# Packed attention and channel mixer: keys and queries turned by TensorE, scores and packed values in small tiles, w1 float32 on chip, the folded w1 made 512 columns ahead

## The chip, the cores and the metric

The kernel runs on one core of one Trainium2 chip. The metric is the device time of one execution in microseconds (us). Engines are TensorE (PE; PEld is its weight load), VectorE (DVE), ScalarE (ACT), GpSimd (POOL) and SyncE (SP), whose queue issues all transfers here.

## The reference

```python
def _attn_ref(q, k, v, p):             # 8 batches, 8 heads, 576 tokens, 64 wide; p has 32 packs
    scale = 1.0 / np.sqrt(q.shape[-1])
    def sm_attn(qq, kk, vv):
        s = scale * np.matmul(qq, kk.transpose(0, 1, 3, 2))
        a = np.exp(s - np.max(s, axis=-1, keepdims=True))
        a = a / (np.sum(a, axis=-1, keepdims=True) + 1e-09)
        return np.matmul(a, vv)
    p_packed = sm_attn(p, k, v)
    return sm_attn(q, p_packed, p_packed)

def _moe_ref(x, U, V, w_ch1, w_ch2):   # x: 8 x 576 x 512; U 576 x 32, V 32 x 576
    h = x.transpose(0, 2, 1) @ U @ V
    u = x + h.transpose(0, 2, 1)
    return u + np.maximum(u @ w_ch1, 0.0) @ w_ch2    # w_ch1 512 x 2048, w_ch2 2048 x 512
```

U, V and the two weights reach the kernel as 64-bit floats and are turned into 32-bit ones on the chip.

## The kernel before

**Two stages.** The opening works in 16 units, (batch, half of the heads). It loads k and v, turns k, makes the scores of the packs against the keys, the softmax and the packed values (`ppall`). After `actx.close()` the order is written out by hand: a loop over the 8 batches, and in each over 16 blocks of 128 hidden columns (kt).

**The folded w1.** The second attention gives weights `a` over 32 packs for each of 8 heads. Since x = a times pp, the product pp w1 (256 x 2048 for each batch, "the fold" here) takes the place of w1, and gemm1 multiplies the 256 attention weights per token with it, then gemm2 multiplies the relu with w2.

**Two kinds of multiplication.** `mm3` splits both operands into a float32r high part and the rest, and runs three float32r matmuls. Plain float32 operands are given to TensorE as they are.

**The opening, unit u.** `a_load` fetches k in a layout in which VectorE's 32x32 transpose (`transposed`, L101) can turn it; `a_split` builds block diagonals of p (`bdp`, L313); `a_scores` runs four float32 matmuls of 288 columns against the block diagonal (L322); `a_softmax` takes maximum and Exp (L330, L332); `a_turn` turns the exponentials on TensorE (L342); `a_pack` multiplies all four heads' values at once and picks the diagonal (L358, L362). Between, `convert_w1` makes w1 float32 (L67 to L71), `split_w1` splits it (L123, L124), and `fold` multiplies pairs of heads by w1 for batches 0 to 3 and stores them in DRAM (`wsr`, L393). A scheduler places these instructions on each engine.

**The batch loop.** Each kt has gemm1 (L632, halves of 256 and 320 tokens, evicted by L638 on ScalarE and L640 on VectorE) and gemm2 of the block before (L649). Every second kt `load_wt` fetches 256 folded columns from DRAM and `split_wt` splits them (L452, L453). `attention(b + 2)` is a list of steps of which one runs per kt: turning q on VectorE (L101), splitting it (L180, L181), scores in `mm3` against block diagonals (L192), softmax, turning back (L225), the mixers with U and V (L236, L249). `later` makes the fold for batches 4 to 7 in the loop (L592) and stores it (`wsc`). The last 64 tokens of two batches share one product (`joint`). In batch 0, w2 is converted, one block a kt. TensorE's transposes and `psT`'s two PSUM banks serve all steps of the loop.

## Time and profile before

| | before |
|---|---|
| median of three runs | 874.17 us (870.17 to 874.59) |
| the profiled execution | 876.01 us |
| its span, first to last instruction | 874.2 us |
| granted TensorE clock, mean | 0.982 |
| TensorE busy | 95% |
| VectorE, ScalarE, GpSimd busy | 59%, 43%, 30% |
| moved by DMA | 98.55 MB |

The span is what the trace shows; the execution's own time has 1.8 us around it. Matmuls are pipelined: a record starts before the one ahead of it has ended, so what a matmul costs on TensorE is the distance between two starts, not its duration. Rows of the timeline give start, duration, engine, line, operation and tile ("out<-in"); rows of groups give busy time and mean duration, then the idle time ahead of the group and what ended it.

### The profile page before, as it was taken

Reading aid. Unit: us, or ns where it says so; the run is one execution under the profiler, and the core shown is the slowest. Engines: PE = TensorE matmul, PEld = TensorE weight load, DVE = VectorE, ACT = ScalarE, POOL = GpSimd, SP = SyncE. Lnnn points to the kernel's source line nnn. Section 1 sums busy time; section 2 is a strip of 40 time slices with the busy share of each in tenths; the row PEclk is TensorE's granted clock in tenths of the full one; section 3 lists DMA queues with packets and bytes.
Section 4 is the critical chain, followed back from the end, with each engine's and each line's share of the span. In section 5 each row is a group of like instructions: output and inputs, shape, how many; then the busy total and the mean of one; then the engine's idle time right before and its main releaser. Section 6 shows DMA issues by size and latency. Waiting matters only on the chain.

```text
span 874.2 us, 12574 instructions
## 1 busy us (share of the span) xinstructions
PE 826.7 (95%) x4440; PEld 706.8 (81%) x4440; DVE 512.6 (59%) x1032; ACT 374.0 (43%) x960; POOL 258.6 (30%) x230
## 2 busy tenths in 40 slices
PE   4779889988989999999999999999999999999997
PEld 2557666777879888888888888988888889889886
DVE  7999985889857876478676433443543424432220
ACT  2557576534445554455554332233333322333220
POOL 3302353545343313132233232323242313221110
PEclk9989997999999999999999999999999999999999
DMA  9869775723424444334453103010301120002001
GB/s 318 236 204 330 221 222 187 253 85 121 160 64 123 140 144 130 98 112 126 117 182 85 53 13 112 25 60 17 112 25 63 56 70 25 25 14 95 25 1 60
DMA packets 59998, 98.55 MB, mean 113 GB/s; under 512 B 12192, under 2 KB 36768, under 8 KB 59936
## 3 DMA queue, kind: packets, MB, share of 16 engines
q1 hardware_dynamic: 59936, 97.75, 36.0%
q8 instruction: 35, 0.57, 0.3%
q14 instruction: 27, 0.22, 0.1%
HBM read 71.52 MB, written 26.21 MB: 112 GB/s over the span
## 4 chain that ended last, share of the span: by engine, by line
PE 73%; DVE 17%; DMA 4%; ACT 3%; issue 3%; SPq 0%; POOL 0%; DVEq 0%; ACTq 0%; POOLq 0%
PE o L78 14%; PE o L77 14%; PE o L76 14%; PE h_ps L76 7%; PE h_ps L77 7%; PE h_ps L78 7%; DVE kT L101 3%; DVE os L70 2%; DVE natT L101 2%; DVE os L69 2%; DMA bits<-in_moe_w_ch_dram 2%; PE w_ps L592 2%; DVE os L71 2%; DVE os L68 2%; PE s_ps L322 2%
## 5 line engine op out<-in xcount | busy, mean ns | idle before, releaser
L640 DVE SCALAR_TENSOR_TENSOR hl<-h_ps,hh 128x256 fp32r<-128x256 f32 x256 | 104.1, 418 | 181.1 <-ACT hh L638 145.7
L78 PE MATMUL o<-w2h,hl 128*128 128x512 f32 x512 | 202.1, 395 | 0.0
L76 PE MATMUL o<-w2h,hh 128*128 128x512 f32 x512 | 201.3, 393 | 0.0
L77 PE MATMUL o<-w2l,hh 128*128 128x512 f32 x512 | 200.9, 392 | 0.0
L638 ACT ACTIVATE hh<-h_ps 128x256 fp32r<-128x256 f32 x256 | 96.0, 383 | 234.4 <-PE h_ps L78 231.4
L76 PE MATMUL h_ps<-ah,fold 128*128 128x256 f32 x496 | 149.3, 301 | 6.3 <-DVE hl L640 5.9
L453 POOL TENSOR_TENSOR fold<-fold 128x512 fp32r<-128x512 f32 x62 | 81.2, 1310 | 230.1 <-ACT fold L452 222.6
L77 PE MATMUL h_ps<-al,fold 128*128 128x256 f32 x496 | 146.1, 295 | 0.0
L78 PE MATMUL h_ps<-ah,fold 128*128 128x256 f32 x496 | 145.7, 294 | 0.0
L78 PEld LDWEIGHTS o<-w2h,hl 128*128 128x128 f32 x512 | 96.4, 188 | 21.6
L77 PEld LDWEIGHTS o<-w2l,hh 128*128 128x128 f32 x512 | 96.6, 189 | 17.5
L76 PEld LDWEIGHTS o<-w2h,hh 128*128 128x128 f32 x512 | 96.7, 189 | 16.8
L76 PEld LDWEIGHTS h_ps<-ah,fold 128*128 128x128 f32 x496 | 93.5, 188 | 13.4 <-DVE hl L640 10.3
L77 PEld LDWEIGHTS h_ps<-al,fold 128*128 128x128 f32 x496 | 93.5, 189 | 2.1
L78 PEld LDWEIGHTS h_ps<-ah,fold 128*128 128x128 f32 x496 | 93.3, 188 | 0.0
L181 POOL TENSOR_TENSOR nlo<-natT,nhi 128x576 fp32r<-128x576 f32 x32 | 46.0, 1453 | 115.5 <-ACT nhi L180 115.5
L68 DVE TENSOR_SCALAR os<-os 128x512 f32<-128x512 f32 (+2 forms) x51 | 37.1, 727 | 40.0 <-ACT os L67 39.9
L322 PE MATMUL s_ps<-kT,bdp 128*128 128x288 f32 x128 | 39.3, 457 | 9.4 <-DVE bdp L313 9.2
L180 ACT CAST nhi<-natT 128x576 fp32r<-128x576 f32 x32 | 20.7, 675 | 55.8 <-DVE natT L101 48.6
L124 POOL TENSOR_TENSOR w1l<-os,w1h 128x512 fp32r<-128x512 f32 x16 | 21.4, 1337 | 67.7 <-ACT w1h L123 61.1
L101 DVE STREAM_TRANSPOSE kT<-nat 128x1152 f32<-128x1152 f32 x16 | 37.3, 2329 | 5.7 <-DMA nat<-in_k_dram 5.6
L67 ACT ACTIVATE os<-bits 128x512 f32<-128x512 f32 x48 | 32.3, 674 | 18.9 <-DMA bits<-in_moe_w_ch_dram 14.7
(143 smaller groups left out, 1398.5 us busy)
## 6 DMA issues: line engine op xcount, KB each, us to landing
bits<-in_moe_w_ch_dram SPq DMA_DIRECT2D x48, 512.0 KB, 4.3
nat<-in_k_dram SPq DMA_DIRECT2D x16, 576.0 KB, 5.3
nat<-in_q_dram SPq DMA_DIRECT2D x16, 576.0 KB, 4.4
vt<-in_v_dram SPq DMA_DIRECT2D x16, 512.0 KB, 5.6
wsr<-fold SPq DMA_DIRECT2D x32, 256.0 KB, 3.8
out_dram<-bits SPq DMA_DIRECT2D x16, 512.0 KB, 3.0
wsc<-bits SPq DMA_DIRECT2D x64, 128.0 KB, 2.2
fold<-wsc SPq DMA_DIRECT2D x32, 256.0 KB, 2.8
```

The costliest lines, as they stand in the source:

```text
L67: nc.scalar.activation(t, high.bitcast(F32), AF.Abs)
L68: nc.vector.tensor_single_scalar(t, t, LEAST, op=ALU.max)
L76: nc.tensor.matmul(ps, lhsT=lh, rhs=rh, start=start, stop=False)
L77: nc.tensor.matmul(ps, lhsT=lh, rhs=rl, start=False, stop=False)
L78: nc.tensor.matmul(ps, lhsT=ll, rhs=rh, start=False, stop=stop)
L101: nc.vector.transpose(t.rearrange("p h (i c) -> p c h i", c=NB), nat.rearrange("p (c h l) -> p c h l", h=2, l=32),)
L124: nc.gpsimd.tensor_tensor(lo, x, hi.bitcast(F32), op=ALU.subtract)
L181: nc.gpsimd.tensor_tensor(lo[:, dh], t, hi[:, dh].bitcast(F32), op=ALU.subtract)
L322: nc.tensor.matmul(s_ps[:, hf, :288], lhsT=bdp[b % 2][:, 2 * g + dh], rhs=kT[:, dh, 288 * hf:288 * hf + 288], start=dh == 0, stop=dh == 1)
L453: nc.gpsimd.tensor_tensor(lo, raw, hi.bitcast(F32), op=ALU.subtract)
L638: nc.scalar.activation(hi, src, AF.Relu)
L640: nc.vector.scalar_tensor_tensor(lo, src, 0.0, hi.bitcast(F32), op0=ALU.max, op1=ALU.subtract)
```

## The change

Token order: a token is now (i, c) with 64 i and 9 c, so that blocks of 64 tokens can be turned by TensorE; output stores and U's loads follow that order. k and q come in that layout and are turned by 10 TensorE transposes per unit (`turn`), copied out of PSUM by ScalarE. Scores are eight float32 matmuls per unit, each on a tile of 64 rows and 32 columns of the array (`scores`); packed values are 20 matmuls on tiles of 128x32 (`a_pack`). pp is turned once more per unit (`a_heads`), kept for three batches (`ppT`) and else in DRAM (`ppTd`, 128 KB a batch). w1 stays on chip as float32 (`w1t`, 32 KB a partition); `fold(b, c)` makes 512 columns of pp w1 by eight float32 matmuls on 64x32 tiles, at kt = 2, 6, 10 and 14, and splits them out of PSUM on ScalarE and VectorE. The DRAM buffers of the folded w1, the block diagonals and `later` are gone. The relu of the joint tokens is stored as float32 and split before the joint product (`joint_parts`).

```diff
+    HALF = (slice(0, 5 * I), slice(5 * I, S))
+    LAST = slice(4 * I, 5 * I)
...
+    ppT = {}
+    ppTd = [dram.tile([P, 2 * P], F32, name=f"ppTd{b}", tag=f"ppTd{b}") for b in range(B)]
...
+    w1t = [pipe.tile([P, DF], F32, name=f"w1t{x}", tag=f"w1t{x}") for x in range(4)]
...
+    chunks = [(x, c) for c in range(NPC) for x in range(4)]
...
+    def convert_w1(n):
+        x, c = chunks[n]
+        float32_of(conv_tile(I32), conv_tile(F32), bits.pop(("w1", n)), w1t[x][:, QW * c:QW * c + QW])
...
+    def load_nat(x, src, b, g):
+        nc.sync.dma_start(
+            out=x.rearrange("p (h y) -> p h y", h=2),
+            in_=src[b, 4 * g:4 * g + 4].rearrange("(h z) (i c) d -> (z i) h (c d)", z=2, c=NT))
...
+    def turn(t, x, h, bank):
+
+        x = x.rearrange("p (h y) -> p h y", h=2)
+        t_ps = bank()
+        if h < 2:
+            for j in range(4):
+                o = P * (2 * (j % 2) + j // 2)
+                nc.tensor.transpose(t_ps[:, o:o + P], x[:, h, P * j:P * j + P], ident)
+            nc.scalar.copy(t[:, 2 * h:2 * h + 2, :4 * I].rearrange("p z (j i) -> p j z i", j=4),
+                           t_ps.rearrange("p (j z i) -> p j z i", j=4, z=2))
+        else:
+            for h in range(2):
+                nc.tensor.transpose(t_ps[:64, P * h:P * h + P], x[:, h, SM:], ident)
+            nc.scalar.copy(t[:64, :, LAST], t_ps[:64, :2 * P].rearrange("p (h i) -> p h i", h=4))
+
+    def scores(lT, t, g, bank):
+
+        ss = [bank() for _ in range(2)]
+        for h in range(4):
+            hs = slice(32 * h, 32 * h + 32)
+            for r in range(2):
+                rs = slice(64 * r, 64 * r + 64)
+                n = HALF[r].stop - HALF[r].start
+                nc.tensor.matmul(ss[r][hs, :n], lhsT=lT[rs, g, hs], rhs=t[rs, h, :n], start=True, stop=True)
+        return [ss[r][:, :HALF[r].stop - HALF[r].start] for r in range(2)]
...
-        def load(g):
-            st["nat", g] = load_nat(pipe, 1, q, b, g)
...
-        def turn_q(g):
-            st["t", g] = transposed(pipe.tile([P, 2, S], F32, name="natT", bufs=1), st["nat", g])
-            st["q", g] = tuple(pipe.tile([P, 2, S], F32R, name=f"n{x}", bufs=1) for x in ("hi", "lo"))
...
-        def scores(g, hf):
-            hi, lo = st["q", g]
-            bqh, bql = st["bq"]
...
-            s_ps = psT.tile([P, 512], F32, name="s_ps", tag="t")
-            ns = slice(288 * hf, 288 * hf + 288)
-            for dh in range(2):
-                j = 2 * g + dh
-                mm3(s_ps[:, :288], (bqh[:, j], bql[:, j]), (hi[:, dh, ns], lo[:, dh, ns]), dh == 0, dh == 1)
-            nc.vector.transpose(st["e", g][:, 9 * hf:9 * hf + 9], s_ps[:, :288])
+        def load():
+            for g in range(2):
+                x = x_tile()[:, :2 * S]
+                load_nat(x, q, b, g)
+                st["x", g] = x
...
+        def turn_q(g, h):
+            if h == 0:
+                st["t", g] = pipe.tile([P, 4, 5 * I], F32, name="xT", bufs=1)
+            turn(st["t", g], st["x", g], h, bank)
+
+        def scores_q(g):
+            e = st["e", g] = pipe.tile([P, S // 32, 32], F32, name="e", bufs=1)
+            s0, s1 = scores(ppT[b], st["t", g], g, bank)
+            nc.vector.transpose(e[:, :10], s0)
+            nc.vector.transpose(e[:, 10:], s1)
 
...
         def mix2(g, hf):
             ah, al = res[b]
             aT = st["aT", g]
-            ns = slice(288 * hf, 288 * hf + 288)
-            v_ps = psT.tile([P, 512], F32, name="v_ps", tag="t")
-            nc.tensor.matmul(v_ps[:, :288], lhsT=st["ms"][:, g * P:(g + 1) * P], rhs=vs[:, ns], start=True, stop=True)
-            nc.vector.tensor_tensor(aT[:, ns], v_ps[:, :288], aT[:, ns], op=ALU.add)
+            ns = HALF[hf]
+            v_ps = bank()[:, :ns.stop - ns.start]
+            vc = vs.rearrange("p (i c) -> p c i", c=NT)
+            lhsT = st["ms"][:, g * P:(g + 1) * P]
+            nc.tensor.matmul(v_ps[:, :4 * I], lhsT=lhsT,
+                             rhs=vc[:, hf:8 + hf:2].rearrange("p (y x) i -> p x y i", x=2), start=True, stop=True)
...
+    def fold(b, c):
+        f_ps = [bank() for _ in range(2)]
+        for x in range(4):
+            xs = slice(32 * x, 32 * x + 32)
+            for g in range(2):
+                gs = slice(64 * g, 64 * g + 64)
+                nc.tensor.matmul(f_ps[g][xs], lhsT=ppT[b][gs, g, xs], rhs=w1t[x][gs, QW * c:QW * c + QW],
+                                 start=True, stop=True)
+        for a in range(2):
+            hi, lo = (pipe.tile([P, 2, QW // 2], F32R, name=f"wt{x}", tag=f"wt{x}", bufs=3) for x in "hl")
+            cs = slice(QW // 2 * a, QW // 2 * a + QW // 2)
+            for g in range(2):
+                nc.scalar.copy(hi[:, g], f_ps[g][:, cs])
+                nc.vector.tensor_tensor(lo[:, g], f_ps[g][:, cs], hi[:, g].bitcast(F32), op=ALU.subtract)
+            wt[b, 2 * c + a] = hi, lo
...
         if g == 0:
-            ua[u]["p"] = sA.tile([P, 2, D], F32, name="pn")
-            nc.sync.dma_start(out=ua[u]["p"], in_=p[b].rearrange("(g h) n d -> (h n) g d", g=2))
-        ua[u]["nat"] = load_nat(sA, 3, k, b, g)
+            pn[b] = sA.tile([P, 2, 2, D], F32, name="pn")
+            for z in range(2):
+                nc.sync.dma_start(out=pn[b][:, :, z], in_=p[b].rearrange("(g h) n d -> (h n) g d", g=2))
+        ua[u]["x"] = sA.tile([P, 2 * S], F32, name="kx", bufs=3)
+        load_nat(ua[u]["x"], k, b, g)
 
...
         b, g = UN[u]
         if g == 0:
-            pn = ua[u]["p"]
-            nc.gpsimd.tensor_scalar_mul(pn, pn, scale)
+            a_p(b)
+        ua[u]["t"] = sA.tile([P, 4, 5 * I], F32, name="kT")
+        for h in range(3):
+            turn(ua[u]["t"], ua[u]["x"], h, bank_a("k"))
+
+    def a_scores(u):
+        b, g = UN[u]
+        ua[u]["s"] = scores(pT[b], ua[u]["t"], g, bank_a("s"))
...
+        for r in range(2):
+            nc.vector.tensor_reduce(mx[:, r:r + 1], ss[r], axis=AX.X, op=ALU.max, negate=True)
+        nc.vector.tensor_tensor(mx[:, 2:], mx[:, :1], mx[:, 1:2], op=ALU.min)
+        e1 = ua[u]["e"] = sA.tile([P, S], F32, name="e1")
+        for r in range(2):
+            nc.scalar.activation(e1[:, HALF[r]], ss[r], AF.Exp, bias=mx[:, 2:], accum_out=sm[:, r:r + 1])
...
+    def a_pack(u):
...
+        p_ps = bank_a("m")()
+        vk = vt[:, :4].rearrange("p h x -> p (h x)").rearrange("p (h k d) -> p k h d", h=4, k=4)
+        for kk in range(5):
+            rows = P if kk < 4 else I
             for h in range(4):
                 hs = slice(32 * h, 32 * h + 32)
-                nc.vector.transpose(bdp[b % 2][hs, :, hs], pn[hs].rearrange("p g (e l) -> p (g e) l", l=32))
-        ua[u]["kT"] = transposed(sA.tile([P, 2, S], F32, name="kT"), ua[u]["nat"])
-
-    def a_scores(u):
+                rhs = vk[:, kk, h] if kk < 4 else vt[:rows, 4, D * h:D * h + D]
+                nc.tensor.matmul(p_ps[hs, :D], lhsT=eT[:rows, kk, hs], rhs=rhs, start=kk == 0, stop=kk == 4)
+        two = ua[u]["two"] = sA.tile([P, 2, D], F32, name="two")
+        nc.scalar.activation(two, p_ps[:, :D].unsqueeze(1).to_broadcast([P, 2, D]), AF.Copy, scale=ua[u]["rs"])
+        nc.gpsimd.tensor_copy(ppall[:, b, g], two[:, 0])
...
-        for hf in range(2):
-            for dh in range(2):
-                nc.tensor.matmul(s_ps[:, hf, :288], lhsT=bdp[b % 2][:, 2 * g + dh], rhs=kT[:, dh, 288 * hf:288 * hf + 288],
-                                 start=dh == 0, stop=dh == 1)
...
-        for kk in range(4):
-            nc.tensor.matmul(pp_ps, lhsT=eT[:, kk], rhs=vm[:, kk], start=kk == 0, stop=False)
-        nc.tensor.matmul(pp_ps, lhsT=eT[:64, 4], rhs=vt[:64, 4].rearrange("p (h d) -> p h d", h=4), start=False, stop=True)
...
-    def fold(r, pr):
-
-        wh, wl = w1t[pr]
-        for c in range(4):
-            cs = slice(512 * c, 512 * c + 512)
-            w_ps = psA.tile([P, 512], F32, name="w_ps", bufs=3)
-            mm3(w_ps, (lwh[r][:, pr], lwl[r][:, pr]), (wh[:, cs], wl[:, cs]), True, True)
...
+        if g == 0:
+            pps[b] = ppT_tile() if b == 0 else sA.tile([P, 2, P], F32, name="ppTa")
+        z_ps = bank()
+        nc.tensor.transpose(z_ps[:, :P], ua[u]["two"].rearrange("p z d -> p (z d)"), ident)
+        nc.scalar.copy(pps[b][:, g], z_ps[:, :P])
+        if g == 1:
+            if b == 0:
+                ppT[0] = pps[0]
             else:
-                nc.scalar.copy(st, w_ps)
-            nc.sync.dma_start(out=wsr[r][P * pr:P * pr + P, cs], in_=st)
...
-    def split_wt(i):
-        raw = raws.pop(i)
-        if i < 2:
-            hl = pipe.tile([P, 2, 2, QW], F32R, name="wt0", tag="vt", bufs=2)
-            hi, lo = hl[:, 0], hl[:, 1]
-        else:
-            hi, lo = (fold_tile(F32R).rearrange("p (g x) -> p g x", g=2) for _ in range(2))
-        nc.scalar.copy(hi, raw)
-        nc.gpsimd.tensor_tensor(lo, raw, hi.bitcast(F32), op=ALU.subtract)
-        wt[pieces[i]] = hi, lo
...
+        if i >= 5:
+            for _ in range(2):
+                if first:
+                    first.pop(0)()
...
+        if i == 14:
+            fold(0, 0)
+        if i == 16:
+            steps = attention(1, res)
+            steps.pop(0)()
...
-                if hf == 1:
-                    parts.append((h_ps[:, 256:320], hjh[:, kj, self.js], hjl[:, kj, self.js]))
-                for (src, hi, lo) in parts:
-                    nc.scalar.activation(hi, src, AF.Relu)
-                for (src, hi, lo) in parts:
-                    nc.vector.scalar_tensor_tensor(lo, src, 0.0, hi.bitcast(F32), op0=ALU.max, op1=ALU.subtract)
+                    mm3(h_ps[:, :ns.stop - ns.start], (wh[:, g, ks], wl[:, g, ks]),
+                        (self.ah[:, g, ns], self.al[:, g, ns]), g == 0, g == 1)
+                ms = slice(4 * I * r, 4 * I * r + 4 * I)
+                src = h_ps[:, :4 * I]
+                nc.scalar.activation(hh[:, ms], src, AF.Relu)
+                if r == 0:
+                    nc.scalar.activation(hj[:, jslot(self.b, kt), self.js], h_ps[:, LAST], AF.Relu)
...
-            if done and kt % 2 == 0 and kt > 0:
-                pr, cc = done.pop(0)
-                folds[pr][5](cc)
+            if steps and kt % 4 != 2:
+                steps.pop(0)()
...
-            if kt % 2 == 0:
-                i = b * NPC + kt // 2
-                if i + 2 < len(pieces):
-                    load_wt(i + 2)
-                if i > 0 and i + 1 < len(pieces):
-                    split_wt(i + 1)
...
+            if kt % 4 == 2 and (b, kt) != (B - 1, NK - 2):
+                n = b * NPC + kt // 4 + 1
+                fold(n // NPC, n % NPC)
+            elif steps:
                 steps.pop(0)()
             if kt == 1:
                 cur.blocks()
             if kt == 3:
                 cur.add_u()
-            if kt == 12:
+            if ahead and kt == 13:
                 ahead.pop(0)()
+            if kt == NK - 1 and b % 2 == 1:
+                parts = [joint_parts(b, 0), joint_parts(b, 1)]
...
+    def joint_parts(b, n):
+
+        hi, lo = conv_tile(F32R), conv_tile(F32R)
+        k0 = 4 * n
+        for (dst, src) in ((slice(0, 1), jslot(b, k0)), (slice(1, 4), k0 + 1)):
+            w = dst.stop - dst.start
+            src = hj[:, src:src + w].rearrange("p k x -> p (k x)")
+            cs = slice(P * dst.start, P * dst.stop)
+            nc.scalar.copy(hi[:, cs], src)
+            nc.vector.tensor_tensor(lo[:, cs], src, hi[:, cs].bitcast(F32), op=ALU.subtract)
+        return hi, lo
```

TensorE in the batch loop, between gemm1 of one kt and gemm2 of the one before. The names: `h_ps` is gemm1, `o` gemm2, `w_ps` the fold for later batches. Before:

```order
L77 MATMUL h_ps_2701<-al,fold 128x320
L78 MATMUL h_ps_2701<-ah,fold 128x320
L592 MATMUL w_ps<-w1p,lwh 128x512
L592 MATMUL w_ps<-w1p,lwl 128x512
L592 MATMUL w_ps<-w1p,lwh 128x512
L592 MATMUL w_ps<-w1p,lwl 128x512
L76 MATMUL o<-w2h_1437,hh 128x512
```

Now the fold stands behind gemm2 (`t_ps` is its PSUM bank, `w1t` w1 on chip):

```order
L85 MATMUL o<-w2l_1874,hh 128x512
L86 MATMUL o<-w2h_1873,hl 128x512
L354 MATMUL t_ps<-w1t_80,ppT 32x512 x2
L354 MATMUL t_ps<-w1t_81,ppT 32x512 x2
L354 MATMUL t_ps<-w1t_82,ppT 32x512 x2
L354 MATMUL t_ps<-w1t_83,ppT 32x512 x2
L84 MATMUL h_ps_2806<-ah,wth 128x320
```

The four 128x512 matmuls of 16 places became eight of 32x512 at 31 places, all of them directly ahead of a gemm1.

TensorE in the same loop at the query scores, behind a gemm2. Before, six matmuls of two halves of the head width:

```order
L78 MATMUL o<-w2h_1439,hl 128x512
L76 MATMUL s_ps<-nhi,bqh 128x288
L77 MATMUL s_ps<-nlo,bqh 128x288
L78 MATMUL s_ps<-nhi,bql 128x288
L76 MATMUL s_ps<-nhi,bqh 128x288
L77 MATMUL s_ps<-nlo,bqh 128x288
L78 MATMUL s_ps<-nhi,bql 128x288
L76 MATMUL h_ps_2876<-ah,fold 128x256
```

Now (`xT` are the turned queries, `ppT` the turned packed values):

```order
L86 MATMUL o<-w2h_84,hl 128x512
L221 MATMUL t_ps<-xT,ppT 32x320
L221 MATMUL t_ps<-xT,ppT 32x256
L221 MATMUL t_ps<-xT,ppT 32x320
L221 MATMUL t_ps<-xT,ppT 32x256
L221 MATMUL t_ps<-xT,ppT 32x320
L221 MATMUL t_ps<-xT,ppT 32x256
L221 MATMUL t_ps<-xT,ppT 32x320
L221 MATMUL t_ps<-xT,ppT 32x256
L84 MATMUL h_ps_2021<-ah,wth 128x320
```

The eight belong to four heads and two halves of the tokens; one such group serves a unit, where two groups of six did.

TensorE in the opening, one unit (`kx` are keys, `two` the packed values twice, `pn` the packs). Now:

```order
L205 MATMUL k_ps<-ident,kx 128x128 x8
L228 MATMUL m_ps<-ident,e_322 128x128
L230 MATMUL m_ps<-ident,e_322 64x128
L221 MATMUL s_ps<-kT,pT 32x320 x4
L228 MATMUL m_ps<-ident,e_322 128x128 x3
L221 MATMUL s_ps<-kT,pT 32x256 x4
L210 MATMUL k_ps<-ident,kx 64x128 x2
L451 MATMUL m_ps<-vt,eT 32x64 x20
L461 MATMUL t_ps<-ident,two 128x128
```

The scheduler has put transposes of another unit between the two halves of the scores.

508 lines of the change are left out of this document (184 added, 324 removed).

## The prediction

> **What bounds the kernel now.** I read the page first, then the busy time by stretches, the waits of TensorE, and its timeline. The page gives the span and the profile by fortieths:
>
> ```profile
> span 874.2 us, 12574 instructions
> PE   4779889988989999999999999999999999999997
> ```
>
> TensorE is filled from about the eighth slice on. The first gemm1 (the first stage of the batch loop) starts at 162.6 us (the row's first start), and the last matmul at 869.4 us. So I cut there; columns are busy us of each engine, granted clock, DMA share, GB/s:
>
> ```profile
> L76 PE MATMUL h_ps<-ah,wt x16: 281/310/583, 162.6 to 180.5; 128*128 128x256 f32 x8, 128*128 128x320 f32 x8
> 869.36 0.39 PE L78 MATMUL o<-w2h,hjl 128*128 128x512 f32 x1
> 0.00:162.60 162.60, 129.54 (x524) 93.99 (x525) 137.12 (x244) 94.01 (x235) 56.38 (x64) 0.93 0.79 247
> 162.60:240.00 77.40, 71.52 (x393) 62.20 (x392) 68.11 (x121) 36.64 (x89) 35.42 (x27) 0.96 0.43 141
> 240.00:870.00 630.00, 625.68 (x3526) 550.61 (x3524) 307.40 (x668) 243.02 (x638) 166.82 (x140) 1.00 0.25 75
> PE h_ps L76 <- DVE hl L640: 5.9, 4, 2.0
> ```
>
> There are two programs in one. In the opening stage VectorE is busiest (137.1 of 162.6 us, 84%), with DMA at 0.79 behind it. In the batch loop, 707 us, TensorE never rests after 240 us, and its one wait of note there totals 5.9 us. So an edit in the loop is worth the TensorE time that it adds or takes away, and an edit in the opening what it does to the engine or queue that fills it. What follows the last matmul (4.8 us) stays.
>
> **What the loop costs.** Matmul records overlap, so I price by the distance of starts. The rows are start, duration, instruction:
>
> ```profile
> 541.61 0.28 PE L76 MATMUL h_ps<-ah,fold 128*128 128x256 f32 x1
> ...
> 543.19 0.39 PE L76 MATMUL o<-w2h,hh 128*128 128x512 f32 x1
> 543.42 0.39 PE L77 MATMUL o<-w2l,hh 128*128 128x512 f32 x1
> ...
> 545.95 0.29 PE L76 MATMUL s_ps<-nhi,bqh 128*128 128x288 f32 x1
> ...
> 546.74 0.28 PE L76 MATMUL h_ps<-ah,fold 128*128 128x256 f32 x1
> ```
>
> One kt is gemm1 1.58 us plus gemm2 2.76 us, and six matmuls of query scores take 0.79 us; one 512-wide matmul is 0.23. Neither gemm changes in count or width. The scores go: 7 batches in the loop x 4 x 0.79 = 22.1 us. The products that make w1 for the later batches go too:
>
> ```profile
> L592 PE MATMUL w_ps<-w1p,lwh 128*128 128x512 f32 x32 | 12.8, 400 | 0.4 <-DVE aT L250 0.4
> L592 PE MATMUL w_ps<-w1p,lwl 128*128 128x512 f32 x32 | 12.6, 392 | 0.0
> 586.66 0.60 PE L225 MATMUL t_ps<-ident,aT 128*128 128x128 f32 x4
> 587.01 0.36 PE L76 MATMUL h_ps<-ah,fold 128*128 128x256 f32 x1
> 587.21 0.28 PE L77 MATMUL h_ps<-al,fold 128*128 128x256 f32 x1
> ```
>
> That is 64 x 0.23 = 14.7 us, and 16 transposes at 0.09 (four take 0.35) are 1.4. Removed from the loop: 38.2 us; 707 - 38 = 669 us stay.
>
> **What the loop gains.** (a) Query turns: per group of four heads 10 transposes, now on TensorE. Two bundles of four at 0.43 (0.35 and a first matmul that starts 0.20 instead of 0.12 before its successor) and one of two at 0.3: 1.16 us, x 14 = 16.2. (b) 14 pairs of query scores and (c) 31 folds, each eight float32 matmuls on 64x32 tiles. No row shows such a tile, so I bound it. A float32 matmul on the whole array, and a change of tile shape:
>
> ```profile
> 62.77 2.10 PE L322 MATMUL s_ps<-kT,bdp 128*128 128x288 f32 x8
> 64.71 1.89 PE L358 MATMUL pp_ps<-vt,eT 128*128 128x256 f32 x8
> 66.44 0.63 PE L342 MATMUL t_ps<-ident,e 128*128 128x128 f32 x4
> ...
> 597.15 0.28 PE L236 MATMUL m_ps<-th,ua 128*128 128x256 f32 x1
> 597.27 0.28 PE L236 MATMUL m_ps<-tl,ua 128*128 128x256 f32 x1
> 597.48 0.38 PE L236 MATMUL m_ps<-th,ua 64*128 64x256 f32 x1
> 597.71 0.28 PE L236 MATMUL m_ps<-tl,ua 64*128 64x256 f32 x1
> 597.91 0.39 PE L76 MATMUL h_ps<-ah,fold 128*128 128x256 f32 x1
> 598.14 0.29 PE L77 MATMUL h_ps<-al,fold 128*128 128x256 f32 x1
> ```
>
> Four matmuls stand as eight records: float32 goes through in two passes. Eight passes of 288 take 1.94 us, of 256 1.73 us: 0.845 ns a column and pass, so a pass of 512 is 0.43 us, of 320 0.27, of 256 0.22. Going to 64-row tiles and back makes four distances 0.21, 0.23, 0.20, 0.23 where 0.12 is usual: 0.39 us; I take 0.3 for tiles a quarter as wide, whose weights load faster. The Trainium skill, TensorEngine Tiling (Array Packing), Key Properties, says that a change of tile shape empties the array; the trace agrees (+0.39 us).
>
> If the eight tiles run together, a fold is two passes, 0.86, plus 0.2 for eight starts behind one another and 0.3 for the change: 1.35 us, and a pair of scores 0.54 + 0.2 + 0.3 = 1.05. If they run one after another, a fold is 16 x 0.43 + 0.3 = 7.2 and scores 4.2. I take the near end: eight tiles of 64x32 cover the array exactly once, as one matmul of the rows above does, no two of them the same part, the row halves write different PSUM banks, and all operands lie ready. So 31 x 1.35 = 41.9 and 14 x 1.05 = 14.7. The loop becomes 669 + 16.2 + 41.9 + 14.7 = 742 us, 35 longer. Token transposes, mix1, residuals and joint keep their matmuls; mix2 gains two 64-wide ones a batch and reads vs with a stride of nine, 0 to 3 us in all.
>
> **What else moves in the loop**, at nothing: splitting a fold takes four ScalarE and four VectorE operations of about 0.4 us, two kt before gemm1 reads it; POOL loses the 1.3 us splits of fold. The DRAM round trip of the folded w1 goes, off TensorE's path. The joint's split moves behind gemm2 of the last kt; its second half waits for the first joint matmuls, 12 x 0.23 = 2.8 us each, which cover it. In batch 0 VectorE keeps four conversions a kt; the 13 us that the loop loses now to such waits and to the clock of 0.96 I keep.
>
> **What the opening becomes.** VectorE loses the key transposes and the block diagonals, POOL the w1 split, TensorE the eight folds and the DRAM stores of them:
>
> ```profile
> L101 DVE STREAM_TRANSPOSE kT<-nat 128x1152 f32<-128x1152 f32 x16 | 37.3, 2329 | 5.7 <-DMA nat<-in_k_dram 5.6
> L124 POOL TENSOR_TENSOR w1l<-os,w1h 128x512 fp32r<-128x512 f32 x16 | 21.4, 1337 | 67.7 <-ACT w1h L123 61.1 <-DMA os<-wsr 6.5
> L313 DVE STREAM_TRANSPOSE bdp<-pn 32x128 f32<-32x128 f32 x32 | 9.5, 295 | 0.4
> L345 ACT COPY eT<-t_ps 128x512 f32<-128x512 f32 x16 | 9.3, 581 | 0.8 <-PE t_ps L342 0.6
> L332 ACT ACTIVATE e<-s_ps,mx 128x576 f32<-128x576 f32 x16 | 11.8, 739 | 12.1 <-DVE mx L330 11.9
> L67 ACT ACTIVATE os<-bits 128x512 f32<-128x512 f32 x22 | 14.9, 676 | 15.9 <-DMA bits<-in_moe_w_ch_dram 11.7 <-DVE os L69 2.9 <-POOL w1l L124 1.1
> q1 hardware_dynamic: 59936, 97.75, 36.0%
> ```
>
> VectorE falls from 137 to about 137 - 37 - 9 - 7 = 84 us (7: the query transposes of batch 0). ScalarE has per unit two key copies out of PSUM like L345's 0.58 and one of 0.3, Exp in two pieces 1.3, eT 0.58, w1's 0.68, some 0.9 of small ones: 4.9 us, 16 units 78, with batch 0's attention 89. TensorE, tiles together: turns 1.3, scores 1.05, back-turns 0.65, packing 0.85 (20 matmuls of 64 columns, four at a time: 10 passes of 0.054, and 0.3), the rest 0.25: 4.1 us, with batch 0 about 76 us. So the transfers are next: what must land before gemm2 can run is k and v 18.9 MB, w1 8.4, p twice 1.0, q 1.2, U and V 0.7, ppT 0.9, w2 1.0 by their shapes: 32.2 MB. The queue moved 97.75 MB in 36.0% of 874.2 us, 311 GB/s at full share: 104 us. The bounds are 104 (full share) and 140 (0.74, less than today's 0.79); VectorE, today's limit, reaches 84%, and loads need less handing over, so I take 0.86: 120 us, 43 shorter.
>
> Sum: 120 + 742 + 4.8 = 867 us of span; with 876.0 - 874.2 = 1.8 around it, 868.6, against 876.0 of the profiled execution: -7.5 us. On the median of 874.17 us that is 866.7; I say **867 us**.
>
> **The rivals.** First: the tiles overlap only in pairs. Each matmul's second pass needs the same tile as its first; if TensorE starts matmuls in program order, tile 2's first pass starts only with tile 1's second, and the eight take 9 x 0.43 + 0.3 = 4.2 us, scores 2.2 + 0.3 = 2.5. That is 31 x 2.85 + 14 x 1.45 = 109 us more in the loop, and 6.2 us a unit in the opening (scores 2.5, packing 1.4), with batch 0 about 115 us of TensorE, at 84% 137: 17 more. 867 + 126 = 993 us, slower. For it: pairs of passes in program order in every row above; against: each tile could hold its second pass back by itself, which no row tests. It decides from a fold of 1.6 us on. The Trainium skill, TensorE: Matmul & The Clock Gate, Part 3: Packing small matmuls, says that matmuls start and end strictly in program order and that only weight loads are pulled ahead; by that rule the time is this rival's. No trace here has such tiles to test it.
>
> Second: one tile at a time: 31 x 5.85 + 14 x 3.15 = 225 us in the loop, and 8.9 us a unit (scores 4.2, packing 2.5), 16 of them 142, with batch 0 and the waits of today an opening of 170: 867 + 275 = 1142 us. For it: the 64-row tiles above are run one behind the other; against: those two use the same tile, and these eight do not.
>
> Third: the tiles overlap, but the opening is held at 140 us, because three PSUM tags of two banks tie TensorE to ScalarE's 4.9 us a unit and the order alternates between them: 867 + 20 = 887. For it: L332 waits 11.9 us for VectorE's maximum today, a chain that stays.
>
> **How the numbers follow.** My forecast 0.46 (own range 850 to 884: opening 110 to 132, fold 1.2 to 1.6), the first rival 0.28, the second 0.08, the third 0.12, none of them 0.06. Repeats differ by about 0.5%, so faster means under 869.8 us and slower over 878.5. The forecast's range puts 0.70 of its chance under 869.8, 0.15 between, 0.15 above; the rivals are slower nearly whole, the rest is even. Faster 0.32 + 0.03, same 0.09, slower 0.07 + 0.28 + 0.08 + 0.10 + 0.03 = 0.56. Slower holds more in sum, but over three separate prices; the likeliest single time stays 867. The range runs from 849 to 1003: it leaves out the second rival and the edges.
>
> **What would show it.** Fold's eight matmuls from the first start to the next gemm1: 1.35 us right, 4.2 the first rival, 7.2 the second. The first gemm1 at 115 to 125 us, DMA share there 0.85; at 140 with ScalarE or TensorE as releaser, the third. The loop from there to the last matmul 742 us. Waits of gemm1 for wt, or of a turn for its bank, would mean that the cover named above is missing.

## The result, and the profile after

The changed kernel takes **901.3 us** (median of 4 runs, 901.06 to 902.82) beside 872.2 us for the kernel before on the same chip: a ratio of 1.034, 95% interval 1.030 to 1.038. It is 3.4% slower, where 867 us were forecast. The opening, its hand-over to the loop and the stores all cost more than forecast; the loop apart from its waits came out near.

The page of the changed kernel (span, busy tenths in 40 slices, the queue with its packets, MB and share of sixteen engines):

```profile
span 901.0 us, 14507 instructions
PE   5788983999999999999999999999999999999995
DMA  9999985223110101001100110010001100000001
q1 hardware_dynamic: 38224, 58.16, 23.8%
```

The cut is the same as before: where gemm1 starts, where it waits, and the last matmul. The name `hl` is the low part of the relu: VectorE makes it out of gemm1's PSUM bank, and until it has, the next gemm1 can't write that bank. These are the row of h_ps, TensorE's wait (us, times, longest), and the last row of its timeline:

```profile
L84 PE MATMUL h_ps<-ah,wth x512: 280/302/636, 133.3 to 871.5; 128*128 128x256 f32 x86, 128*128 128x320 f32 x85
PE h_ps L84 <- DVE hl L580: 13.8, 1, 13.8
889.63 0.40 PE L86 MATMUL o<-w2h,os 128*128 128x512 f32 x1
```

Two smaller waits of TensorE stand in the first batch of the loop, for the split of a fold (`wtl`) and for the turned weights (`aT`):

```profile
PE t_ps L221 <- DVE wtl L361: 2.1, 1, 2.1
PE t_ps L228 <- DVE aT L275: 1.2, 1, 1.2
```

And the busy time by stretches (busy us of each engine, granted clock, DMA share, GB/s):

```profile
0.00:133.30 133.30, 105.92 (x1262) 62.76 (x1263) 67.03 (x193) 76.38 (x205) 13.53 (x31) 0.83 1.00 236
140.00:160.00 20.00, 7.95 (x48) 6.61 (x49) 15.37 (x28) 9.25 (x22) 4.33 (x3) 0.66 0.45 137
877.00:889.50 12.50, 12.50 (x62) 10.41 (x61) 2.40 (x5) 1.87 (x5) 0.00 (x0) 1.00 0.13 46
889.70:901.00 11.30, 0.33 (x2) 0.00 (x0) 0.00 (x0) 0.59 (x1) 0.00 (x0) 0.64 0.22 65
```

Up to the first gemm1 the sixteen DMA engines are full on average (share 1.00), yet they move 236 GB/s. The forecast had 311 at full share. Then one wait of 13.8 us stands in the loop. After the last matmul 11.4 us pass instead of 4.8. The stores just ahead of it run at a share of 0.13, which is two engines of sixteen.

| us, profiled execution | before | forecast | after |
|---|---|---|---|
| to the first gemm1 | 162.6 | 120 | 133.3 |
| loop, with its waits | 706.8 | 742 | 756.3 |
| of that, gemm1 waiting for hl | 8.5 | 8.5, kept | 14.0 |
| after the last matmul | 4.8 | 4.8 | 11.4 |
| span | 874.2 | 867 | 901.0 |

Over the forecast: 13.3 + 14.3 + 6.6 = 34.2 us, which is 901.0 less the forecast's sum of 866.8. The wait for hl is counted here over the whole loop: 8.5 us before, where the 5.9 of the prediction's row begin at 188 us. Without its longest wait, 13.8 us, the loop of the changed kernel takes 742.5 us; the experiments below go by that number.

The folds and the query scores in TensorE's timeline (start, duration, instruction):

```profile
484.69 0.39 PE L86 MATMUL o<-w2h,hl 128*128 128x512 f32 x1
485.01 1.09 PE L354 MATMUL t_ps<-w1t,ppT 64*32 64x512 f32 x16
486.03 0.41 PE L84 MATMUL h_ps<-ah,wth 128*128 128x320 f32 x1
486.28 0.31 PE L85 MATMUL h_ps<-al,wth 128*128 128x320 f32 x1
...
158.05 0.40 PE L86 MATMUL o<-w2h,hl 128*128 128x512 f32 x1
158.38 0.76 PE L221 MATMUL t_ps<-xT,ppT 64*32 64x320 f32 x16
159.07 0.41 PE L84 MATMUL h_ps<-ah,wth 128*128 128x320 f32 x1
...
467.09 0.28 PE L86 MATMUL h_ps<-ah,wtl 128*128 128x256 f32 x1
467.50 1.09 PE L221 MATMUL t_ps<-xT,ppT 64*32 64x320 f32 x16
468.52 0.50 PE L84 MATMUL o<-w2h,hh 128*128 128x512 f32 x1
```

Sixteen records (eight matmuls of two passes) take 1.02 us from their first start to the next matmul. The start before them is 0.32 away instead of 0.23, and the first distance behind them is 0.25 instead of 0.15. So a fold is 1.2 us where 1.35 was forecast. The first rival's 4.2 and the second's 7.2 us fall here. The scores, counted in the same way, are 0.9 us between gemm2 and gemm1 and 1.4 between gemm1 and gemm2, where 1.05 was forecast.

What TensorE waits for at 138 to 152 us is VectorE's timeline:

```profile
146.55 0.43 DVE L76 TENSOR_SCALAR os<-os 128x512 f32<-128x512 f32 x1 [1.61 <-ACT os L75]
147.01 0.43 DVE L77 TENSOR_SCALAR os<-os 128x512 int32<-128x512 int32 x1
147.48 0.69 DVE L78 SCALAR_TENSOR_TENSOR os<-bits,os 128x512 int32<-128x512 int32 x1
148.20 0.69 DVE L79 SCALAR_TENSOR_TENSOR os<-bits,os 128x512 int32<-128x512 int32 x1
...
151.58 0.75 DVE L580 SCALAR_TENSOR_TENSOR hl<-h_ps,hh 128x256 fp32r<-128x256 f32 x2
```

The opening's last conversions (four pieces of w1, then two of w2) stand in VectorE's queue ahead of the first hl. VectorE itself waits there for ScalarE's first step of each (L75), and that for the piece's load.

### The profile page after: what moved, and what is told of

Same layout as the page of the kernel before. It is cut to its first block, busy times and chain, and to the rows that moved or that the text cites. A ratio compares the mean times of both kernels' runs of the same rounds, so it can differ in the third digit from the quotient of the medians.

```text
span 901.0 us, 14507 instructions
## 1 busy us (share of the span) xinstructions
PE 842.1 (93%) x5808; PEld 670.3 (74%) x5808; DVE 379.4 (42%) x892; ACT 331.5 (37%) x952; POOL 93.9 (10%) x111
## 4 chain that ended last, share of the span: by engine, by line
PE 80%; DMA 10%; DVE 5%; ACT 2%; issue 1%; SPq 1%; POOL 0%; DVEq 0%; ACTq 0%
PE o L84 15%; PE o L85 15%; PE o L86 15%; PE h_ps L84 8%; PE h_ps L86 7%; PE h_ps L85 7%; DMA bits<-in_moe_w_ch_dram 5%; PE t_ps L354 3%; DMA kx<-in_k_dram 2%; DMA vt<-in_v_dram 2%; PE t_ps L221 2%; PE t_ps L205 1%; DVE os L76 1%; PE t_ps L296 1%; DVE os L78 1%
## 5 line engine op out<-in xcount | busy, mean ns | idle before, releaser
L84 PE MATMUL h_ps<-ah,wth 128*128 128x320 f32 (+1 forms) x512 | 159.4, 311 | 14.0 <-DVE hl L580 14.0
L85 PE MATMUL h_ps<-al,wth 128*128 128x320 f32 (+1 forms) x512 | 152.8, 298 | 0.0
L86 PE MATMUL h_ps<-ah,wtl 128*128 128x320 f32 (+1 forms) x512 | 152.5, 298 | 0.0
L84 PEld LDWEIGHTS h_ps<-ah,wth 128*128 128x128 f32 x512 | 98.0, 191 | 46.1 <-issue 25.7
L85 PEld LDWEIGHTS h_ps<-al,wth 128*128 128x128 f32 x512 | 98.2, 192 | 1.9
L86 PEld LDWEIGHTS h_ps<-ah,wtl 128*128 128x128 f32 x512 | 98.1, 192 | 0.0
L361 DVE TENSOR_TENSOR wtl<-t_ps,wth 128x256 fp32r<-128x256 f32 x128 | 48.5, 420 | 94.3 <-ACT wth L360 91.0
L360 ACT CAST wth<-t_ps 128x256 fp32r<-128x256 f32 x128 | 43.3, 375 | 109.5 <-PE t_ps L354 98.5
L316 POOL TENSOR_TENSOR al<-aT,ah 128x320 fp32r<-128x320 f32 (+1 forms) x32 | 26.3, 823 | 207.1 <-ACT ah L315 207.0
L354 PE MATMUL t_ps<-w1t,ppT 64*32 64x512 f32 x512 | 35.9, 601 | 0.4 <-ACT ppTa L462 0.4
```

The costliest lines, as they stand in the source:

```text
L84: nc.tensor.matmul(ps, lhsT=lh, rhs=rh, start=start, stop=False)
L85: nc.tensor.matmul(ps, lhsT=lh, rhs=rl, start=False, stop=False)
L86: nc.tensor.matmul(ps, lhsT=ll, rhs=rh, start=False, stop=stop)
L316: nc.gpsimd.tensor_tensor(al[:, g, ns], aT[:, ns], ah[:, g, ns].bitcast(F32), op=ALU.subtract)
L354: nc.tensor.matmul(f_ps[g][xs], lhsT=ppT[b][gs, g, xs], rhs=w1t[x][gs, QW * c:QW * c + QW], start=True, stop=True)
L360: nc.scalar.copy(hi[:, g], f_ps[g][:, cs])
```

## The experiments

The theory had three parts. (1) Transfers that cover only 64 partitions (w1's halves L137, v's halves L394) make the loads slow. (2) The conversions hold up hl. (3) The stores run on two engines. Rivals: other transfers running beside them slow the loads; TensorE's and ScalarE's chain bounds the opening; the distance of the rows in DRAM slows the stores.

The diffs of this part are shortened: `a <- b` is a load of a from b. The runs come from several chips, on which the kernel before had medians of 871.2 to 873.9 us, so two or three microseconds between runs say little.

Packet times are counted from the traces: median / mean ns of the packets that start in the stretch. In e7 the 4096 B packets hold GpSimd's half of v too.

```
                      4096 B (w1, w2)   1024 B (v)   stretch, us
before                159 / 206         46 / 52      0 to 163
b1_w1_halves          241 / 253         46 / 55      0 to 163
b2_w1_columns         2 x 84 / 98       46 / 51      0 to 163
after                 278 / 277         78 / 78      0 to 120
e3_w1_rows            179 / 219         75 / 75      0 to 120
e4_v_rows             267 / 272         48 / 58      0 to 120
e5_all_loads          162 / 208         46 / 51      0 to 120
e7_pool_queue         286 / 296         79 / 80      0 to 120
e8_act_queue          279 / 286         74 / 74      0 to 120
e9_v_interleaved      279 / 277         49 / 60      0 to 120
```

**Half the partitions, on the kernel before.** In load_w1:

```diff
-in_=w1[pr * P:(pr + 1) * P, 1024 * cc:1024 * cc + 1024]
+for a in range(2): bits[64 * a:64 * a + 64], w1[pr * P + 64 * a:..., 1024 * cc:1024 * cc + 1024]
```

> The kernel before, with each w1 piece of the opening (128 partitions of 4096 B) loaded by two transfers of 64 partitions instead of one of 128; nothing else differs. Theory A, a transfer that covers 64 of the 128 partitions takes longer for each byte: the 4096 B packets of the opening go from a median of 159 ns to about 268 (what the changed kernel shows), 2048 of them are 8 to 14 us of sixteen engines, and the time goes from 872 to 880 to 886 us. Theory B, the packets were longer in the changed kernel only because other transfers (the keys' 2304 B, the values' rows) ran beside them: the median stays at 150 to 170 ns and the time within 3 us of 872.

874.36 us beside 871.25, a ratio of 1.0035 (1.0012 to 1.0059). The packets did what theory A says (159 to 241 ns, while v's beside them stayed at 46). The time rose by only 3 us, outside the 8 to 14 expected. For most of this opening something else is as full as the transfers; two of its stretches:

```profile
20.00:40.00 20.00, 16.50 (x76) 12.35 (x75) 19.65 (x32) 12.13 (x34) 6.82 (x7) 1.00 1.02 277
80.00:100.00 20.00, 17.74 (x71) 12.40 (x69) 19.62 (x38) 10.71 (x28) 7.31 (x6) 0.91 0.79 224
```

VectorE, the third busy number, is at 19.6 of 20 us in both, and the DMA share is 1.02 in the first and 0.79 in the second. Over the first 162 us the share rose from 0.79 to 0.85, with room left. That the cost of a slow packet is paid only where the loads are the bound fits this, and the larger gain from w1's rows in the changed kernel below.

**As many transfers, but of all partitions.**

```diff
+for a in range(2): bits[:, 512 * a:512 * a + 512], w1[pr * P:(pr + 1) * P, 1024 * cc + 512 * a:...]
```

> The kernel before, with each w1 piece of the opening loaded by two transfers of half the columns, 128 partitions of 2048 B each; nothing else differs. It has as many and as large transfers as two transfers of 64 partitions. Theory A (the 64 partitions are what costs): two packets of 2048 B take about 2 x 84 ns, as one of 4096 B did (159 ns), and the time stays within 3 us of 872. Theory C (two transfers for one cost, whatever they cover): the time rises as with the halves, by 8 us or more.

868.43 us, a ratio of 0.9951 (0.9931 to 0.9972). Two packets of 2048 B take 168 ns, so theory C falls: it isn't the number of transfers. That the kernel becomes 3 us faster was not expected, and why was not tried.

**Whole rows in the changed kernel.** w1 as 128 adjacent rows; v as two heads on 128 partitions instead of four heads on 64; then both, with k and q in one run a partition:

```diff
-for g in range(2): b[64 * g:64 * g + 64] <- w1[4 * D * g + D * x:... + D]
+b <- w1[P * x:P * x + P]
-main = v[...].rearrange("h (i c) d -> i h (c d)"); vt[64 * a:64 * a + 64, :4] <- main[:, :, 4 * D * a:...]
+main = v[...].rearrange("(h z) (i c) d -> (z i) h (c d)", z=2); vt[:, 2 * a:2 * a + 2] <- main[:, :, 4 * D * a:...]
```

> The changed kernel, with each w1 piece loaded by one transfer of 128 adjacent rows onto all 128 partitions; the rows are then not those that the folds want (the result is another), while every instruction and every byte is as before. Theory A, covering half the partitions is what made w1's packets slow: the 4096 B packets fall from 266 ns on average to 160 to 200, which is 8 to 13 us of sixteen engines; the opening of the changed kernel is bound by its loads (a share of 0.95 to 1.09), so the first gemm1 and the end of w1's conversions come 8 to 13 us earlier and the time is 888 to 894 (changed kernel: 901.3). Theory B, the opening is bound by TensorE's and ScalarE's chain between 74 and 100 us and not by the loads: the packets get shorter and the time falls by less than 4 us.

> The changed kernel, with the two main transfers of each piece of v covering 128 partitions and two heads each, instead of 64 partitions and four heads; as many transfers, packets of 1024 B and source rows with the same distance, but the rows stand in other places (the result is another). Theory A (half the partitions): the 1024 B packets fall from 77 ns to about 52, which is 8192 x 25 / 16 = 13 us of sixteen engines, and the time to 888 to 893. Theory D, the rows' distance of 2304 B in DRAM made these packets slow: they stay at 77 ns and the time at 901.

> The changed kernel with both of these, and with k and q in one run of 4608 B a partition instead of two of 2304 B (the result is another). If the sum of the prediction failed by the rate alone, the rate of the opening returns to about 300 GB/s, its 33 MB are loaded by 110 to 115 us, the first gemm1 is at 115 to 122 us instead of 133.3, and the wait for hl shrinks with w1's last pieces coming earlier: time 875 to 884. If the opening is bound elsewhere once the loads are quick (ScalarE, TensorE at a clock of 0.6 to 0.8, the queue of transfers), the first gemm1 stays above 126 and the time above 888.

These three leave rows in places where the kernel doesn't want them; they measure the loads alone. They take 893.19, 885.75 and 878.19 us: 8.1, 15.6 and 23.1 less than the changed kernel, the second 2 us below its range. The packets of the transfer that was changed became quick, the other one's did not: in the table, w1's in the first, v's in the second. Theory A holds for both; B and D fall. The sum of the two, 23.7, is what the third gives, so two runs of 2304 B for k and q cost nothing that shows. The third kernel's h_ps and its waits (us, times), and its opening:

```profile
L84 PE MATMUL h_ps<-ah,wth x512: 280/302/633, 107.4 to 845.0; 128*128 128x256 f32 x86, 128*128 128x320 f32 x85
...
  DVE hl L577: 16.3, 2
```

```profile
0.00:107.40 107.40, 92.16 (x1262) 56.19 (x1263) 65.63 (x193) 73.41 (x204) 13.56 (x31) 0.94 0.96 293
```

Up to there it has the same matmuls, weight loads and VectorE instructions, but 293 GB/s, and the first gemm1 at 107.4, 26 us earlier and 8 us earlier than I had expected. The wait for hl did not shrink with it but grew to 16.3. Quick packets don't shorten the conversions: each piece waits for its load (ScalarE's longest wait there is 4.8 us for one), ScalarE and VectorE in turn, and the raw pieces share two buffers (`bits`).

**Both halves under way at once.** The halves for partitions 64 to 127 issued by another engine, for v and w1 alike; first GpSimd, then ScalarE (nc.scalar):

```diff
-nc.sync.dma_start(out=vt[64 * a:64 * a + 64, :4], ...)
+(nc.sync, nc.gpsimd)[a].dma_start(out=vt[64 * a:64 * a + 64, :4], ...)
```

> The changed kernel, with the transfers that fill partitions 64 to 127 (of each w1 piece and of v's main part) issued by GpSimd, the ones for partitions 0 to 63 by SyncE as before; shapes, bytes and results are the same. Theory A1, the 64 partitions of one half have a way into the chip's memory that is narrower than sixteen engines: two halves under way at once use both ways, the 4096 B and 1024 B packets come near 160 to 200 and 50 to 60 ns, the opening gains most of what the two kernels with whole rows gained (8 and 15 us), and the time is 880 to 888 (changed kernel: 901.3). Theory A2, the cost sits in each transfer of 64 partitions by itself (its share for each engine is short), whatever runs beside it: packets and time stay as they are, 898 or more, or the time rises because GpSimd's own queue of work waits behind its transfers.

> As the run before, with ScalarE issuing the transfers for partitions 64 to 127 in place of GpSimd. Theory A1: the same gain in the packets; but ScalarE then stands still where a transfer's buffer is not yet free (the conversion of w1 two pieces before, the packing of v), and the exponentials and copies queued behind it are late, so the time is 882 to 900. Theory A2: 901 or more.

903.86 and 905.91 us, with packets within 6% of the changed kernel's (74 to 79 ns against 78, 279 to 286 against 278). In the second run two or more packets of each queue's halves were in flight together for 26% of the first 120 us. With eight or more of SyncE's beside them, ScalarE's 1024 B packets took 78 ns, and with none 72. So a second half under way brings nothing, and A1 falls in both. That fits what the Trainium skill says in DMA: Bandwidth & Descriptors, Rules for kernel authors: two transfers to the two partition halves go through the same sixteen engines either way, and one transfer of 128 partitions is to be used.

**The same 64 partitions, spread.** In turn, for k alone, the copy out of PSUM writes its columns to match:

```diff
-vt[64 * a:64 * a + 64, :4] <- main[:, :, 4 * D * a:4 * D * a + 4 * D]
+vt[a:P:2, :4]              <- main[:, :, 4 * D * a:4 * D * a + 4 * D]
+to.rearrange("p z (k i a) -> p k a z i", k=2, a=2) <- t_ps.rearrange("p (k a z i) -> p k a z i", k=2, a=2, z=2)
```

> The changed kernel, with the two main transfers of each piece of v filling every second partition (0, 2, 4 ... and 1, 3, 5 ...) instead of the lower and the upper 64; bytes, packets of 1024 B, source rows and number of transfers are the same. The keys' turned copy writes its columns two by two to match (one copy by ScalarE as before, with steps of 8 B), and the result is the reference's. Theory F, engines that write partitions close together stand in each other's way: spread over all 128 partitions the 1024 B packets fall from 77 to 50 to 58 ns and the time by about the 15.6 us that v's 128 partitions gave: 884 to 890. Theory A2, 64 partitions are slow wherever they lie: the packets stay at 74 to 80 ns and the time at 899 to 905.

891.26 us, 10.0 less. The packets fell from 78 to 49 ns, as theory F has it, and the first gemm1 came at 123.0; the time missed F's range by 1.3 us. Two heads on 128 partitions had gained 15.6 us; what the other 5.6 are was not tried. So for v's packets it is not how many partitions but where they lie; w1 was not tried in this way. The Trainium skill, SBUF — State Buffer, Door 1: The DMA port swizzle (why [64,N] ≈ [32,N]), gives a map: partitions 0 to 63 reach eight of sixteen ports of the on-chip memory, 64 to 127 the other eight. By that map every second partition reaches all sixteen, and the measured packets agree. Why two halves at once on two queues gained nothing, though the map puts them on different ports, stays open.

**The stores.**

```diff
-out[self.b].rearrange("(i c) m -> c i m", c=NT)[c0:c0 + 5:4], in_=os_[:, a]
+for z in range(2): out[self.b].rearrange("(i c) m -> c i m", c=NT)[j + 2 * a + 4 * z], in_=os_[I * z:I * z + I, a]
```

> The changed kernel, with each output store of two times 64 rows issued as two stores of 64 rows; the rows and their places are the same. Theory A, a transfer is dealt to the DMA engines by its outermost dimension, which is 2 in the changed kernel's stores, so that two engines carry one: with 64 as the outermost dimension the last stores go out at over 100 packets of 2048 B a microsecond instead of 25, the time from the last matmul to the end falls from 11.4 to about 5 us, and the time from 901.3 to about 895. Theory B, the rows of 2 KB lying 18 KB apart in DRAM are what is slow: the rate stays at 25 a microsecond and the time at 901.

894.55 us, 6.8 less. The stretches up to the last matmul and from there to the end:

```profile
876.00:888.00 12.00, 12.00 (x60) 9.99 (x59) 2.40 (x5) 1.43 (x4) 0.00 (x0) 1.00 0.36 84
888.10:893.00 4.90, 0.43 (x2) 0.00 (x0) 0.00 (x0) 0.59 (x1) 0.00 (x0) 0.84 0.23 54
```

The tail is 5.0 us with the rows as far apart as they were, so theory A holds and B falls. The packets agree: 25 start in a microsecond, two in flight, in the changed kernel's last stores, and about 100 with sixteen in flight in this run's. The rule is in the Trainium skill, DMA: Bandwidth & Descriptors, Why a DMA increments its semaphore by 16 and not by 1: the number of engines is the largest up to 16 that divides the slowest dimension of both patterns. The store's is 2 (two values of c), and the changed kernel's share of 0.13 agrees.

**The conversions moved into the loop.** some_w1 stops at 12 of 16, and the first batch's steps convert one w1 piece and one w2 piece each:

```diff
-        if n_w1 < 16:
+        if n_w1 < 12:
+    seq = [w2 2, w1 12, w2 3, w1 13, w2 4, w1 14, w2 5, w1 15, w2 6, w2 7, ...]
```

> The changed kernel, with the last four of w1's sixteen pieces (n = 12 to 15, the columns that the first batch's fold 3 reads at kt = 10) loaded and converted in the first batch's steps kt = 1 to 4, between w2's, instead of in the opening. Theory A, the 13.8 us wait of the first products for hl is VectorE's queue holding these conversions, whose loads were the opening's last: the wait falls under 1 us, the opening has 2.1 MB less to load (8.6 us at 245 GB/s), the loop stays near 742 us, and the time goes from 901.3 to 879 to 888 us. Theory B, the work only moves: the conversions (some 3 us of VectorE each) and their loads push back hl or w2's pieces in steps 1 to 5, and the time stays above 895.

895.04 us: 6.3 less, outside A's range and just inside B's. The wait for hl fell only to 6.1 us, now in four waits, as conversions of w2 and w1 still stand between one hl and the next, and the first gemm1 came 4.1 us earlier, not 8.6. Without the wait the loop was 745.3 us, 2.8 more than before the move. Part of what left the opening came back.

**Four places of the array instead of eight.**

```diff
-lhsT=ppT[b][64 * g:..., g, xs], rhs=w1t[x][64 * g:...]
+lhsT=ppT[b][64 * (x % 2):..., g, xs], rhs=w1t[2 * g + x // 2][64 * (x % 2):...]
```

> The changed kernel, with each w1 piece loaded by one transfer of 128 adjacent rows, and the folds reading them there: head 4g + x then lies in the row half x % 2 for both g, so that the eight products of a fold use four places of the array (row half, 32 columns), two for each, instead of eight. Theory A, products on different places of the array run at once and those on one place one after the other: a fold takes twice its 1.0 us, 31 us more over the 31 folds of the loop, less what w1's quicker packets give (8 to 13 us): 919 to 925. Theory E, the fold is short because each product of 32 columns is short by itself, whatever its place: the fold stays at 1.0 us and the time is that of the kernel with the quick w1 alone.

921.5 us, inside A's 919 to 925. The fold:

```profile
492.14 1.94 PE L353 MATMUL t_ps<-w1t,ppT 64*32 64x512 f32 x16
494.02 0.41 PE L84 MATMUL h_ps<-ah,wth 128*128 128x320 f32 x1
```

1.88 us in place of 1.02, with the same shapes and the same order. Products on different places run at once, those on one place one after the other; theory E falls. The records one by one show how. With eight places, eight passes start 0.007 us apart from 485.01 on, and the other eight from 485.47 on. With four, groups of four start at 492.14, 492.60, 493.03 and 493.46. With w1 loaded in the same way on eight places the time was 893.2, 28.3 us less. In the seven later batches, where nothing else differs, it is 22.7 us for 27 folds, 0.84 each; the rest lies in the opening and the first batch.

**Together.** Stores of 64 rows; three of four w1 pieces as 128 adjacent rows with the heads so placed that eight places are still used; eight w1 pieces in the loop. The first row gives first partition, first head and number of heads of each transfer, the second the tile and the row half of each head:

```diff
+(((0, 0, 2),), ((0, 2, 2),), ((0, 5, 2),), ((0, 7, 1), (64, 4, 1)))[x]
+y, z = ((0, 0), (0, 1), (1, 0), (1, 1), (3, 1), (2, 0), (2, 1), (3, 0))[4 * g + x]
```

> The changed kernel with the stores of 64 rows, three of every four w1 pieces loaded as 128 adjacent rows (the fourth in two halves; the folds read head 4g + x where its rows then lie, still in eight places of the array), and the last eight of w1's pieces loaded and converted in steps kt = 1 to 8 of the first batch; all results are those of the reference. By the single runs: stores 6.8 us; w1's rows three quarters of 8.1 on half of the pieces, 3 us; eight pieces out of the opening twice the 6.3 us of four, 12.6: 901.3 - 22.4 = 879, a range of 872 to 888. If the pieces in the loop push back hl or w2 there: 888 to 900.

887.01 us, 8 over the middle of what I expected and inside its range. The opening gained 14.3 us (first gemm1 at 119.0) and the tail 5.7, but the loop without its wait of 8.4 became 752.5: ten us came back there. Then v on every second partition as well:

> The combined kernel (887.0 us: stores of 64 rows, w1's adjacent rows, eight pieces of w1 in the loop) with v on every second partition as well. Theory F: 14 us of sixteen engines less in an opening that is bound by its loads, 872 to 878. Theory A2: 885 to 890.

871.03 us, 1 us under theory F's range, a ratio of 0.998 (0.996 to 1.000) to the kernel before; gemm1 starts at 105.0. And with only four pieces in the loop, one in every second step:

> The second combined kernel (871.0 us) with four of w1's pieces (n = 12 to 15) instead of eight in the loop, one in every second step (kt = 1, 3, 5, 7). In the second combined kernel VectorE was busy 17 of 20 us from 120 to 180 us and TensorE stood still for hl, wtl and aT there: its way from the first gemm1 to the last matmul was 760 us where 742.5 is the changed kernel's without its wait. Theory G, two conversions in one step are more than VectorE has room for: the four in the opening cost 7 us of loads (2.1 MB at 300 GB/s) and the loop gets back 8 to 14: 863 to 870. Theory H, the conversions cost the same wherever they stand: 871 to 878.

**863.82 us**, a ratio of 0.990 (0.987 to 0.993) to the kernel before, 37.5 us under the changed kernel, with the same result. Its h_ps and its last matmul; then a stretch of its loop, and the same stretch of the second combined kernel:

```profile
L84 PE MATMUL h_ps<-ah,wth x512: 274/302/614, 106.0 to 840.4; 128*128 128x256 f32 x86, 128*128 128x320 f32 x85
858.50 0.40 PE L86 MATMUL o<-w2h,os 128*128 128x512 f32 x1
```

```profile
108.00:180.00 72.00, 58.98 (x352) 47.72 (x352) 60.26 (x111) 34.06 (x84) 23.29 (x24) 0.93 0.36 119
```

```profile
108.00:180.00 72.00, 55.23 (x317) 43.78 (x317) 60.52 (x114) 31.91 (x77) 16.85 (x14) 0.91 0.39 120
```

Four pieces more in the opening cost 1.0 us there (106.0 against 105.0), and the loop with its waits fell from 760.1 to 752.5. All of that is in the first batch: from the second on, the loop takes 649 us in both, as in the changed kernel. VectorE is as busy in that stretch in both (60 of 72 us), but TensorE gets 35 more instructions through. Its waits there for wtl and aT fell from 9.6 us to 5.9, and those for hl from 7.6 to 7.1. Theory G holds in its sign and time, though not in its price of 7 us for the opening. Whether fewer pieces or their wider spacing did it is not told apart.

## Why the prediction was wrong

**The loop** came out near in its prices and not in its total: 756.3 us against 742. The forecast's 742 holds the loop's old waits ("the 13 us that the loop loses now to such waits and to the clock of 0.96 I keep"), so the agreement of 742.5 without the longest wait is in part luck. Of the 14.3 us too many, 5.5 are more waiting for hl (14.0 against 8.5), and 4.0 are TensorE's waits for wtl and aT, which the forecast had at nothing. The other 5 were not followed up. The two open prices were near: 1.2 us for a fold (forecast 1.35), and 0.9 or 1.4 for scores (forecast 1.05). That the eight tiles run together because they "cover the array exactly once" was argued there; the run with four places shows it. The Trainium skill's rule (TensorE: Matmul & The Clock Gate, Part 3), by which the first rival had 993 us, does not hold for these passes: all eight first passes start before any second one, 0.007 us apart.

**The opening's rate is the step that failed.** "The queue moved 97.75 MB in 36.0% of 874.2 us, 311 GB/s at full share: 104 us" takes the rate of the old transfers for the new ones, as if bytes alone set it. The share of 0.86 was too low (1.00), the rate at full share much too high (236). That is 13.3 of the 34.2 us. Two transfers that the change halved, w1's and v's, are why: with whole rows the rate is 293 GB/s and gemm1 starts at 107, before the 120 that I took and near my bound of 104. That halves of the partitions could cost anything was not weighed.

**The hand-over was in the sum only at its old size.** I summed VectorE's work (84 us, measured 67) and stopped there. Its order was not read: the last w1 and w2 conversions stand ahead of the first hl, each a chain of load, ScalarE and four VectorE steps, and cost 13.8 us in one wait. The waits were 16.3 in all with quick loads, so this is a second error, not the first one again.

**The stores**: "what follows the last matmul (4.8 us) stays" held the tail for untouched, while the change rewrote the stores' pattern. It was 11.4 us.

**The third rival** (opening held at 140 us by ScalarE and the PSUM tags) came nearest in time and not in cause: the opening was full of transfers.

## What to carry to other kernels

Price a load by its shape, not by its bytes. Which partitions it covered set how long a packet took (46 against 78 ns), and its outermost dimension how many engines carried it (two against sixteen). Here two adjacent halves in place of whole rows cost 23 us, more than the 10 that the last kernel gains on the one before. Where a stage hands over to the next, read the order of the engine's queue as well as its sum. And ask of each slower transfer whether its stage is bound by transfers: w1's halves cost 3 us in one kernel and 8 in the other.

## What the runs showed of the hardware

- A packet of 4096 B took 159 to 179 ns in a transfer of 128 partitions and 241 to 279 in one of 64 adjacent ones; 1024 B took 46 to 48 and 74 to 79. On every second partition 1024 B took 49.
- A store of two times 64 rows had two engines, 46 GB/s at a share of 0.13; the tail after the last matmul was 11.4 us, and 5.0 as single stores of 64 rows.
- Eight float32 matmuls of 512 columns on eight 64x32 places took 1.02 us together, on four places 1.88.
- Loading w1 in two halves of its columns, all partitions each, made the kernel before 0.5% faster; the cause was not tried.
